# A filter, two mixtures of experts, one planned program: the order of the last layer's slots and a third count product

## The chip, the cores and the metric

One core of one Trainium2 chip runs the whole program in one launch. The metric is device time in microseconds; the median of 3 runs of the kernel before is 1300.23 us (1297.22 to 1307.93).

## The reference

The input x has shape (4, 2496, 256). Three stages follow each other:

1. A filter: a real FFT along the 2496 positions, a product with a complex filter, the inverse FFT. Its output is taken as 9984 tokens of 256 numbers.
2. A first mixture of 8 experts (256 to 1024, relu, 1024 to 256) with greedy capacity. All 9984 x 8 logits are sorted; from the largest down, each free token goes to that expert unless the expert already holds 1248 tokens. 8 x 1248 = 9984, so at the end every expert is full.
3. A second mixture of 8 experts of the same sizes: each token goes to the expert with the largest cosine similarity, and its output is scaled by the softmax weight. There is no capacity, so these experts get unequal numbers of tokens.

```python
logits = x @ w_gate
for idx in np.argsort(-logits.flatten()):
    tok, e = (int(idx) // E, int(idx) % E)
    if assigned[tok] >= 0 or counts[e] >= cap:
        continue
    assigned[tok] = e
    counts[e] += 1
...
expert_idx = np.argmax(logits2, axis=1)
out[mask] = gate_w[mask, None] * (np.maximum(x[mask] @ w1[e], 0.0) @ w2[e])
```

## The kernel before

**Stages.** `Fft` does the filter and writes the tokens to `xs` in memory. `Moe.layers` (from L1576) then works through a fixed list of 46 items, one after the other, on TensorE (PE). An item is a block of up to 512 token rows for one expert: its rows are transposed (L989), multiplied by the expert's first matrix in eight chunks (L1006), passed through relu (L1009 on ScalarE, the remainder L1012 on VectorE), and multiplied by the second matrix (L1024), two chunks behind. All matrices are split into a high and a low part (L957 on ScalarE, L958 on VectorE), because every product is made of three float32r products.

**Items, counted from 0, in the kernel before.** Items 0 to 16 are the first mixture's easy part: expert "full" in three blocks, then the seven "known" experts with 2 x 384 rows each. Then come the seven "late" blocks of 480 rows (the rest of each expert), mixed with "slots". A slot is 512 rows of one expert of the second mixture; which expert and which rows is read from a table on the chip. The order is: late 1 and 2 (items 17, 18), four slots slA (19 to 22), late 3 and 4 (23, 24), three slots slC (25 to 27), late 5, 6, 7 (28 to 30), five slots slM (31 to 35), eight slots slB (36 to 43), two half slots slS (44, 45). With the reference's inputs these slots hold every token, and the general loops of `rest` (L1693) don't run: the trace has 84 scatters into `out`, 20 x 4 + 2 x 2.

**The search.** Which tokens belong to a late block is known only when the greedy phases are done (`Greedy.phase`, L729; seven searches `Greedy.search`, L515). Phase k ends with the expert's number `ei` (L802). A search is a chain of small VectorE steps with a TensorE product between them, which adds counts over partitions: four coarse products (L535), one of the coarse remainder `sg` (L561), two of 63 thresholds (L576).

**The lists.** For each block `compact` (L864) turns a mask into row numbers `ids` and flags `val` (L908, L910). `Moe.listing` calls it in order: full, known 1 to 7, late 1 to 7. Known lists wait until the item is at most `SOON` ahead; late lists are made as soon as their expert is known. GpSimd (POOL) then gathers the rows (L1204), two items ahead.

**Routes and tables.** When the items of a group (an entry of `full + known` or of `late`) have left TensorE, `route` (L1359) finds the second mixture's expert for up to 12 tiles of 128 tokens and scatters their rows with GpSimd into `ys` (L1435). Behind certain groups `table_a` (L1292) makes the next table: it looks for experts with 512 rows not taken yet. Groups are routed one after the other. After the last group come `table_b` (L1312), `pads` (16 scatters of filler rows) and `table_s`. A slot's weights (L940, L950) and rows (L1213) are loaded through SP's queue once its table is there, the rows of slB only when the pads are done.

**What sets the order.** The program is written out by a planner in Python that keeps an estimated clock for TensorE, ScalarE and VectorE. In `beside` (L1647), after each piece of TensorE work, it lets background generators take a step: rows and weights, then `routes`, `lists` and `greedy`, as long as VectorE's estimated backlog is small. If TensorE's next item needs something that isn't planned yet, `need` (L1613) pulls the generator until it is there. The rows of item n + 1 are needed when item n has had its fourth chunk (`columns`, called for c in (3, 5)), its weights when it starts. Each engine then executes its part in the order so written.

Of the kernel before, what the change touches and what calls it, by code (L numbers as in the profile page):

```python
# [11 lines left out]
F32 = mybir.dt.float32  # L12
F32R = mybir.dt.float32r
F16 = mybir.dt.float16
# [4 lines left out]
ALU = mybir.AluOpType  # L19
AX = mybir.AxisListType  # L20
# [6 lines left out]
CAP = 1248  # L27
# [6 lines left out]
LATE = CAP - CUT  # L34
# [9 lines left out]
G0 = 42  # L44
SLACK = 1.5
SOON = 8

GT = 12
BEHIND = 2
# [380 lines left out]
class Greedy:  # L430
# [84 lines left out]
    def search(s, mh):  # L515


        nc, c = s.nc, s.c
        V = nc.vector
        need = c['st'][:, 2 * NLEV + 1, :]  # L520
        junk = s.t([128, 702], F16, "m2")
        junk2 = s.t([128, 702], F16, "junk2")
        thr = s.t([128, 3], F32, "thr", bufs=3)
        V.tensor_copy(thr, c['st'][:, 2 * NLEV, :])
        for k in range(NLEV):
            cn = s.t([128, 3], F16, "cn", bufs=2)
            with nc.allow_low_precision(reason="integer counts up to 702 are exact in float16"):
                nc.scalar.activation(junk2, mh, AF.Sign, bias=thr[:, 2:3], scale=1.0, accum_out=cn[:, 2:3])
                for j in (0, 1):
                    V.tensor_scalar(junk, mh, thr[:, j:j + 1], None, op0=ALU.is_ge, op1=ALU.add, accum_out=cn[:, j:j + 1])  # L530
            D = s.t([128, 3], F32, "D", bufs=2)
            V.tensor_tensor(D, thr, c['st'][:, NLEV + k, :], ALU.add)
            yield (1.5, 0.2, 0.87) if k == 0 else (1.65, 0.4, 0.87)
            pc = s.P([128, 3], F32, "gs")
            nc.tensor.matmul(pc, c['o16'], cn, start=True, stop=True)  # L535
            ge = s.t([128, 3], F32, "ge", bufs=2)
            sc = s.t([128, 1], F32, "sc", bufs=2)
            V.scalar_tensor_tensor(ge, pc, 1.0, need, op0=ALU.mult, op1=ALU.is_ge, accum_out=sc)
            th2 = s.t([128, 3], F32, "thr", bufs=3)
            V.scalar_tensor_tensor(th2, c['st'][:, k, :], sc, D, op0=ALU.mult, op1=ALU.add)  # L540
            thr = th2

        base = s.t([128, 1], F32, "Tb")
        up = s.t([128, 1], F32, "Tu")
        sg = s.t([128, 1], F16, "sg")
        V.tensor_scalar(base, thr[:, 0:1], -5.0, None, op0=ALU.add)
        V.tensor_scalar(up, base, -1.0, -4.5, op0=ALU.mult, op1=ALU.add)
        with nc.allow_low_precision(reason="integer counts up to 702 are exact in float16"):
            nc.scalar.activation(junk2, mh, AF.Sign, bias=up, scale=1.0, accum_out=sg)
        yield (0.6,)  # L550
        m2 = s.t([128, 702], F32, "m2")
        V.scalar_tensor_tensor(m2, mh, base, s.K3.rearrange("p a b -> p (a b)"), op0=ALU.subtract, op1=ALU.add)
        yield (0.95,)
        V.scalar_tensor_tensor(m2, m2, 5.0, m2, op0=ALU.is_lt, op1=ALU.mult)
        yield (0.9,)
        top = s.t([128, 8], F32, "top")
        V.max(top, m2)
        yield (0.9, 0.0, 0.87)
        nd = s.t([128, 1], F32, "nd")
        pa = s.P([128, 1], F32, "gs")  # L560
        nc.tensor.matmul(pa, c['o16'], sg, start=True, stop=True)  # L561
        V.tensor_scalar(nd, pa, -0.5, float(CAP - 8 * 702), op0=ALU.mult, op1=ALU.add)
        s.T = s.t([128, 1], F32, "T")
        V.memset(s.T, 1.0)
        for k in range(2):
            th = s.t([128, 63], F32, "th")
            V.tensor_scalar(th, c['j63'], 2.0 ** (-4 - 6 * k), s.T, op0=ALU.mult, op1=ALU.add)
            cm = s.t([128, 63, 8], F16, "cc")
            V.tensor_tensor(cm, top[:, None, :].to_broadcast([128, 63, 8]), th[:, :, None].to_broadcast([128, 63, 8]), ALU.is_ge)
            yield (0.8,)  # L570
            cn = s.t([128, 63], F16, "cn6")
            with nc.allow_low_precision(reason="integer counts up to 8 are exact in float16"):
                V.tensor_reduce(cn, cm, axis=AX.X, op=ALU.add)
            yield 0.6
            pc = s.P([128, 63], F32, "gs")
            nc.tensor.matmul(pc, c['o16'], cn, start=True, stop=True)  # L576
            sc = s.t([128, 1], F32, "sc", bufs=2)
            V.tensor_scalar(th, pc, nd, None, op0=ALU.is_ge, op1=ALU.add, accum_out=sc)
            V.scalar_tensor_tensor(s.T, sc, 2.0 ** (-4 - 6 * k), s.T, op0=ALU.mult, op1=ALU.add)
        s.cnt = s.t([128, 1], F32, "cnt")  # L580
        V.tensor_scalar(th[:, 0:8], top, s.T, None, op0=ALU.is_ge, op1=ALU.add, accum_out=s.cnt)
        V.scalar_tensor_tensor(s.cnt, sg, 0.5, s.cnt, op0=ALU.mult, op1=ALU.add)
        V.tensor_scalar(s.cnt, s.cnt, 351.0, None, op0=ALU.add)

        s.ok = s.t([128, 1], F32, "ok")
        V.tensor_scalar(s.ok, base, 0.0, None, op0=ALU.is_gt)
        s.ov = s.t([128, 1], F32, "ov")
        V.scalar_tensor_tensor(s.ov, top[:, 7:8], 1.0, s.ok, op0=ALU.is_ge, op1=ALU.mult)
        V.tensor_tensor(s.T, s.T, base, ALU.add)
        V.tensor_scalar(s.T, s.T, 1024.0, None, op0=ALU.mult)  # L590
# [438 lines left out]
class Moe:  # L1029
# [2 lines left out]
    NA = 4  # L1032
    NC = 3
    NM = 5
    NB = 8
    NS = 2
    NX = 48

# [19 lines left out]
    def listing(s):  # L1058
        g = s.greedy
        yield from g.compact(("full", 0), *g.first, CAP)  # L1060
        for k in range(1, NE):
            yield from s.wait_for(g.ei, ("known", k), s.G)
            while s.it < 2 * k + 1 - SOON and not s.force:
                yield 1.0
            yield from g.known(k)
        for ph in range(1, NE):
            yield from s.wait_for(g.ei, ("late", ph), s.G)
            yield from g.late(ph)

    def wait_for(s, got, key, gen):  # L1070
# [370 lines left out]
    def plan(s):  # L1441
        nc, d = s.nc, s.d
        s.items, s.sets = [], []
        V = nc.vector

        def known1(key):
            def f():
                yield from s.wait_for(s.greedy.ei, key, s.G)
                return s.greedy.ei[key][0:1]
            return f  # L1450

        def known2(name, k):
            def f():
                yield from s.table_ready(name)
                return getattr(s, name)[0:1, 0, k:k + 1]
            return f

        def place(name, k):
            def f():
                yield from s.table_ready('padded' if name == 'slB' else name)  # L1460
                return getattr(s, name), k
            return f


        full = [[(("full", 0), FULL)]]
        known = [[(("known", k), KNOWN) for k in range(a, min(a + 2, NE))] for a in (1, 3, 5, 7)]
        late = [[(("late", k), (LATE,)) for k in q] for q in ((1, 2), (3, 4), (5, 6, 7))]
        s.st = {}
        ng = itertools.count()

        def first(groups):
            for lists in groups:
                g, t = next(ng), 0
                for key, parts in lists:
                    s.sets.append(dict(i0=len(s.items), known=known1(key), w1=d['w1m'], w2=d['w2m'], w2x=d['w2x'], engs=(V, V)))
                    k = 0
                    for T in parts:
                        n = [128] * (T // 128) + [T % 128] * (T % 128 > 0)
                        s.items.append(dict(set=len(s.sets) - 1, x=[], list=key, k=k, g=g, t=t, n=n, last=False))
                        k += len(n)  # L1480
                        t += len(n)
                s.items[-1]['last'] = True

        def slots(name, N, w):
            for k in range(N):
                s.sets.append(dict(i0=len(s.items), known=known2(name, k), w1=d['w1n'], w2=d['w2n'], w2x=None, engs=(V, V)))
                s.items.append(dict(set=len(s.sets) - 1, x=[], place=place(name, k), n=[128] * w))

        first(full + known)
        n = len(full + known)  # L1490
        s.tables = {n - 2: ('slA', s.NA), n: ('slC', s.NC), n + 1: ('slM', s.NM)}
        for k, name, N in ((0, 'slA', s.NA), (1, 'slC', s.NC), (2, 'slM', s.NM)):
            first(late[k:k + 1])
            slots(name, N, 4)
        slots('slB', s.NB, 4)
        slots('slS', s.NS, 2)
        s.groups = next(ng)

    def done1(s, q, t, m, last=False):
# [502 lines left out]
```

## Time and profile before

| | |
|---|---|
| median of 3 runs | 1300.23 us (1297.22, 1300.23, 1307.93) |
| profiled execution | 1316.35 us |
| its span in the trace | 1314.6 us |
| TensorE busy | 1219.6 us, 93% of the span |
| VectorE, ScalarE, GpSimd busy | 65%, 51%, 33% |
| mean granted TensorE clock | 0.971 |

How to read it: TensorE's matmuls are pipelined, so its busy share shows where it had work, and not that it ran at its peak. A slice or window in which its busy time or its granted clock falls is one in which it waited. ScalarE's first relu of an item is a good mark of the item's start, since there are eight per item in a fixed order; the distance between two such marks is what an item took.

### The profile page before, as it was taken

To read this page: it belongs to the slowest core of one execution; us is meant where nothing else is said; L and a number is where in the kernel's file an instruction comes from. 1 tells how busy PE (TensorE), PEld (TensorE's weight loads), DVE (VectorE), ACT (ScalarE), POOL (GpSimd) and SP (SyncE) were. 2 spreads that over 40 slices of the span, in tenths; PEclk is the share of its full clock that TensorE was granted. 3 is DMA by queue.
4 is the path that set the end of the run, shared out by engine and by line. 5 is a ranking of instruction groups with operands and counts; after the bars stand their busy time and mean duration, and the time that the engine had idled before them with its cause. 6 is when DMAs were issued, how large, how long until landed. Compare 5 with 4: busy or idle time off the path is not lost.

```text
span 1314.6 us, 23468 instructions
## 1 busy us (share of the span) xinstructions
PE 1219.6 (93%) x7893; PEld 1057.5 (80%) x7893; DVE 858.0 (65%) x2061; ACT 665.2 (51%) x1407; POOL 429.8 (33%) x955
## 2 busy tenths in 40 slices
PE   7998999699999989989899999987899899999996
PEld 7565545489999989989788999876799899999996
DVE  2578767578787877887767778763456464445543
ACT  2666656455465564554455456433454444545443
POOL 1334300303363533736147221621114731211112
PEclk9998999799999999999999999997899999999998
DMA  7876667541243322421545443422533654443420
GB/s 238 253 237 216 208 209 223 176 125 47 68 130 91 111 74 57 132 86 57 154 143 180 129 130 114 125 90 76 159 116 126 195 163 130 140 146 131 126 91 24
DMA packets 124044, 178.26 MB, mean 136 GB/s; under 512 B 29383, under 2 KB 88763, under 8 KB 123645
## 3 DMA queue, kind: packets, MB, share of 16 engines
q1 hardware_dynamic: 111131, 143.33, 36.1%
q0 software_dynamic: 12480, 33.17, 7.4%
q8 instruction: 64, 1.05, 0.3%
q14 instruction: 79, 0.65, 0.2%
q10 hardware_dynamic: 290, 0.07, 0.0%
HBM read 137.32 MB, written 39.99 MB: 135 GB/s over the span
## 4 chain that ended last, share of the span: by engine, by line
PE 48%; DVE 7%; issue 4%; POOL 2%; ACT 2%; DMA 1%; POOLq 0%; DVEq 0%; ACTq 0%
PE kp_b L1024 23%; PE kp_a L1006 23%; PE kp_a L989 2%; DVE k_hl L1012 2%; DVE k_w1l L958 1%; DMA k_xg<-xs,g_ids 1%; ACT k_hh L1009 1%; POOL ys L1435 0%; POOL out L1435 0%; DVE k_w L958 0%; ACT g_le L899 0%; POOL k_xg L1204 0%; DVE g_m L530 0%; ACT k_w1h L957 0%; DMA k_raw<-w1m 0%
## 5 line engine op out<-in xcount | busy, mean ns | idle before, releaser
L1024 PE MATMUL kp_b<-k_w,k_hh 128*128 128x256 f32 (+2 forms) x2624 | 505.5, 289 | 3.1 <-ACT k_y L1506 3.1
L1024 PEld LDWEIGHTS kp_b<-k_w,k_hh 128*128 128x128 f32 (+1 forms) x2624 | 422.0, 190 | 17.1 <-ACT k_y L1506 3.7
L1009 ACT ACTIVATE k_hh<-kp_a 128x512 fp32r<-128x512 f32 (+3 forms) x368 | 201.4, 548 | 433.8 <-PE kp_a L1006 350.5
L1012 DVE SCALAR_TENSOR_TENSOR k_hl<-kp_a,k_hh 128x512 fp32r<-128x512 f32 (+3 forms) x368 | 228.4, 624 | 247.3 <-ACT k_hh L1009 196.1
L1024 PE MATMUL kp_b<-k_w,k_hl 128*128 128x256 f32 (+2 forms) x1312 | 372.3, 284 | 1.7 <-DVE g_oth L836 1.0
L1006 PE MATMUL kp_a<-k_xh,k_w1h 128*128 128x512 f32 (+3 forms) x736 | 274.0, 373 | 9.8 <-DVE k_hl L1012 6.0
L1006 PE MATMUL kp_a<-k_xl,k_w1h 128*128 128x512 f32 (+3 forms) x736 | 274.0, 373 | 0.9 <-issue 0.9
L1024 PEld LDWEIGHTS kp_b<-k_w,k_hl 128*128 128x128 f32 (+1 forms) x1312 | 248.1, 189 | 1.5 <-DVE g_oth L836 1.2
L1006 PE MATMUL kp_a<-k_xh,k_w1l 128*128 128x512 f32 (+3 forms) x736 | 213.5, 371 | 5.3 <-DVE k_w1l L958 5.3
L1435 POOL DMA_INDIRECT out<-k_xg,k_y x84 | 88.5, 1054 | 281.0 <-ACT k_xg L1523 262.4
L1006 PEld LDWEIGHTS kp_a<-k_xh,k_w1h 128*128 128x128 f32 x736 | 140.6, 191 | 21.0 <-DVE k_hl L1012 7.2
L1006 PEld LDWEIGHTS kp_a<-k_xh,k_w1l 128*128 128x128 f32 x736 | 137.3, 190 | 23.4 <-DVE k_w1l L958 6.1
L1006 PEld LDWEIGHTS kp_a<-k_xl,k_w1h 128*128 128x128 f32 x736 | 140.3, 191 | 11.3 <-issue 1.7
L1204 POOL DMA_INDIRECT k_xg<-xs,g_ids x80 | 84.8, 1060 | 180.6 <-issue 117.8
L958 DVE TENSOR_TENSOR k_w<-k_raw,k_w 128x1024 fp32r<-128x1024 f32 (+2 forms) x75 | 91.5, 1222 | 14.5 <-ACT k_w L957 11.3
L958 DVE TENSOR_TENSOR k_w1l<-k_raw,k_w1h 128x1024 fp32r<-128x1024 f32 x74 | 90.2, 1224 | 14.0 <-ACT k_w1h L957 13.4
L1435 POOL DMA_INDIRECT ys<-k_y,m_pi x80 | 83.2, 1040 | 33.4 <-POOL m_sp L1434 18.3
L302 POOL TENSOR_TENSOR v<-sw,ff 128x512 f32<-128x512 f32 x40 | 50.9, 1273 | 97.1 <-ACT sw L300 96.5
L1507 POOL COPY m_L<-k_y 128x8 f32<-128x8 f32 x80 | 19.2, 262 | 190.9 <-ACT k_y L1506 188.5
L957 ACT CAST k_w<-k_raw 128x1024 fp32r<-128x1024 f32 (+2 forms) x75 | 78.5, 1049 | 0.0
L957 ACT CAST k_w1h<-k_raw 128x1024 fp32r<-128x1024 f32 x74 | 76.4, 1042 | 2.4 <-DMA k_raw<-w1m 2.4
L992 DVE TENSOR_TENSOR k_xl<-kp_a,k_xh 128x512 fp32r<-128x512 f32 (+3 forms) x92 | 56.9, 619 | 24.3 <-ACT k_xh L991 24.2
(344 smaller groups left out, 1504.3 us busy)
## 6 DMA issues: line engine op xcount, KB each, us to landing
k_raw<-w1n SPq DMA_DIRECT2D x44, 512.0 KB
k_raw<-w2n SPq DMA_DIRECT2D x44, 512.0 KB
k_raw<-w1m SPq DMA_DIRECT2D x30, 512.0 KB
k_raw<-w2m SPq DMA_DIRECT2D x30, 512.0 KB
k_y<-ys SPq DMA_DIRECT2D x84, 132.0 KB
ff<-ff SPq DMA_DIRECT2D x40, 256.0 KB
xs<-yt SPq DMA_DIRECT2D x42, 234.0 KB
w2m<-w2mt SPq DMA_DIRECT2D x16, 512.0 KB
```

The costliest lines, as they stand in the source:

```text
L302: nc.gpsimd.tensor_tensor(r2(v), r2(sw), bc(ff[:, 256:512]), ALU.mult)
L957: s.nc.scalar.copy(hi, src)
L958: f = lambda: eng.tensor_tensor(lo, src, hi.bitcast(F32), ALU.subtract)
L989: nc.tensor.transpose(p[:, 128 * k:128 * k + n], tt[:n, 128 * c:128 * c + 128], s.ident[:n, :n])
L992: late(lambda: nc.vector.tensor_tensor(b, p[:, :T], a.bitcast(F32), ALU.subtract), T)
L1006: nc.tensor.matmul(p[:, :T], w[:, c, f0:f0 + 128], x[:, c, :T], start=q == 0, stop=q == 5)
L1009: nc.scalar.activation(hh[:, :T], p[:, :T], AF.Relu)
L1012: nc.vector.scalar_tensor_tensor(o, a, 0.0, b, op0=ALU.max, op1=ALU.subtract), T, (id(H), f))
L1024: nc.tensor.matmul(p[:m, :n], h[:, t0:t0 + m], w[:, f, :], start=f == 0 and q == 0 and (n > 256 or b % 2 == 0), stop=f == 7 and q == 2 and ...
L1204: s.nc.gpsimd.indirect_dma_start(out=x[:m], out_offset=None, in_=s.d['xs'], in_offset=bass.IndirectOffsetOnAxis(ap=ids[:m], axis=0))
L1435: st = s.nc.gpsimd.indirect_dma_start(out=out, out_offset=bass.IndirectOffsetOnAxis(ap=idx, axis=0), in_=src, in_offset=None, **k)
L1507: nc.gpsimd.tensor_copy(q['L2'][:m, :, t:t + 1], y[:m, 256:264][:, :, None])
```

## The change

It does three things. In `search` the product of `sg` is no longer made by itself: `sg` is copied into a 64th column beside the 63 counts, and the need `nd` is read from that column of the first of the two products. In `listing` a late list is made only when its item is at most `LSOON` = 5 ahead. In `plan` the late groups become (1, 2), (3, 4), (5, 6), (7), so there is one more route; two of the five slM slots come ahead of late 5; and behind group (5, 6) a fourth table slN of two slots is made, which leaves six slots for slB. The order is then: late 1, 2 (17, 18), slA (19 to 22), late 3, 4 (23, 24), slC (25 to 27), slM (28, 29), late 5, 6, 7 (30 to 32), slM (33 to 35), slN (36, 37), slB (38 to 43), slS (44, 45).

```diff
--- before.py
+++ after.py
@@ -44,6 +44,7 @@
 G0 = 42
 SLACK = 1.5
 SOON = 8
+LSOON = 5
 
 GT = 12
 BEHIND = 2
@@ -555,11 +556,8 @@
         yield (0.9,)
         top = s.t([128, 8], F32, "top")
         V.max(top, m2)
-        yield (0.9, 0.0, 0.87)
+        yield (1.0,)
         nd = s.t([128, 1], F32, "nd")
-        pa = s.P([128, 1], F32, "gs")
-        nc.tensor.matmul(pa, c['o16'], sg, start=True, stop=True)
-        V.tensor_scalar(nd, pa, -0.5, float(CAP - 8 * 702), op0=ALU.mult, op1=ALU.add)
         s.T = s.t([128, 1], F32, "T")
         V.memset(s.T, 1.0)
         for k in range(2):
@@ -568,14 +566,17 @@
             cm = s.t([128, 63, 8], F16, "cc")
             V.tensor_tensor(cm, top[:, None, :].to_broadcast([128, 63, 8]), th[:, :, None].to_broadcast([128, 63, 8]), ALU.is_ge)
             yield (0.8,)
-            cn = s.t([128, 63], F16, "cn6")
+            cn = s.t([128, 64], F16, "cn6")
+            V.tensor_copy(cn[:, 63:64], sg)
             with nc.allow_low_precision(reason="integer counts up to 8 are exact in float16"):
-                V.tensor_reduce(cn, cm, axis=AX.X, op=ALU.add)
+                V.tensor_reduce(cn[:, 0:63], cm, axis=AX.X, op=ALU.add)
             yield 0.6
-            pc = s.P([128, 63], F32, "gs")
+            pc = s.P([128, 64], F32, "gs")
             nc.tensor.matmul(pc, c['o16'], cn, start=True, stop=True)
             sc = s.t([128, 1], F32, "sc", bufs=2)
-            V.tensor_scalar(th, pc, nd, None, op0=ALU.is_ge, op1=ALU.add, accum_out=sc)
+            if k == 0:
+                V.tensor_scalar(nd, pc[:, 63:64], -0.5, float(CAP - 8 * 702), op0=ALU.mult, op1=ALU.add)
+            V.tensor_scalar(th, pc[:, 0:63], nd, None, op0=ALU.is_ge, op1=ALU.add, accum_out=sc)
             V.scalar_tensor_tensor(s.T, sc, 2.0 ** (-4 - 6 * k), s.T, op0=ALU.mult, op1=ALU.add)
         s.cnt = s.t([128, 1], F32, "cnt")
         V.tensor_scalar(th[:, 0:8], top, s.T, None, op0=ALU.is_ge, op1=ALU.add, accum_out=s.cnt)
@@ -1032,7 +1033,9 @@
     NA = 4
     NC = 3
     NM = 5
-    NB = 8
+    MFIRST = 2
+    NN = 2
+    NB = 6
     NS = 2
     NX = 48
 
@@ -1060,11 +1063,13 @@
         yield from g.compact(("full", 0), *g.first, CAP)
         for k in range(1, NE):
             yield from s.wait_for(g.ei, ("known", k), s.G)
-            while s.it < 2 * k + 1 - SOON and not s.force:
+            while s.it < s.wanted["known", k] - SOON and not s.force:
                 yield 1.0
             yield from g.known(k)
         for ph in range(1, NE):
             yield from s.wait_for(g.ei, ("late", ph), s.G)
+            while s.it < s.wanted["late", ph] - LSOON and not s.force:
+                yield 1.0
             yield from g.late(ph)
 
     def wait_for(s, got, key, gen):
@@ -1464,7 +1469,7 @@
 
         full = [[(("full", 0), FULL)]]
         known = [[(("known", k), KNOWN) for k in range(a, min(a + 2, NE))] for a in (1, 3, 5, 7)]
-        late = [[(("late", k), (LATE,)) for k in q] for q in ((1, 2), (3, 4), (5, 6, 7))]
+        late = [[(("late", k), (LATE,)) for k in q] for q in ((1, 2), (3, 4), (5, 6), (7,))]
         s.st = {}
         ng = itertools.count()
 
@@ -1481,19 +1486,25 @@
                         t += len(n)
                 s.items[-1]['last'] = True
 
-        def slots(name, N, w):
-            for k in range(N):
+        def slots(name, ks, w):
+            for k in ks:
                 s.sets.append(dict(i0=len(s.items), known=known2(name, k), w1=d['w1n'], w2=d['w2n'], w2x=None, engs=(V, V)))
                 s.items.append(dict(set=len(s.sets) - 1, x=[], place=place(name, k), n=[128] * w))
 
         first(full + known)
         n = len(full + known)
-        s.tables = {n - 2: ('slA', s.NA), n: ('slC', s.NC), n + 1: ('slM', s.NM)}
-        for k, name, N in ((0, 'slA', s.NA), (1, 'slC', s.NC), (2, 'slM', s.NM)):
-            first(late[k:k + 1])
-            slots(name, N, 4)
-        slots('slB', s.NB, 4)
-        slots('slS', s.NS, 2)
+        s.tables = {n - 2: ('slA', s.NA), n: ('slC', s.NC), n + 1: ('slM', s.NM), n + 2: ('slN', s.NN)}
+        first(late[:1])
+        slots('slA', range(s.NA), 4)
+        first(late[1:2])
+        slots('slC', range(s.NC), 4)
+        slots('slM', range(s.MFIRST), 4)
+        first(late[2:])
+        slots('slM', range(s.MFIRST, s.NM), 4)
+        slots('slN', range(s.NN), 4)
+        slots('slB', range(s.NB), 4)
+        slots('slS', range(s.NS), 2)
+        s.wanted = {z['list']: k for k, z in reversed(list(enumerate(s.items))) if 'list' in z}
         s.groups = next(ng)
 
     def done1(s, q, t, m, last=False):
```

## Rows read from the trace of the kernel before

**Rows 1.** the page, part 1: engine, busy us (share of the span), instructions
```profile
PE 1219.6 (93%) x7893; PEld 1057.5 (80%) x7893; DVE 858.0 (65%) x2061; ACT 665.2 (51%) x1407; POOL 429.8 (33%) x955
```

**Rows 2.** waits of PE over the span: us in total, times, longest
```profile
PE kp_a L989 <- DMA k_xg<-xs,g_ids: 23.5, 11, 8.6
```

**Rows 3.** one window: PE, PEld, DVE, ACT, POOL busy, granted clock, DMA share, GB/s
```profile
885.00:900.00 15.00, 4.78 (x22) 3.54 (x22) 3.61 (x23) 2.33 (x10) 3.88 (x4) 0.55 0.37 112
```

**Rows 4.** ScalarE timeline, first relu of items 28, 29, 30, 31, 36 and 37
```profile
874.07 0.57 ACT L1009 ACTIVATE k_hh<-kp_a 128x480 fp32r<-128x480 f32 x1 [2.11 <-PE kp_a L1006]
...
918.12 0.56 ACT L1009 ACTIVATE k_hh<-kp_a 128x480 fp32r<-128x480 f32 x1
...
947.32 0.57 ACT L1009 ACTIVATE k_hh<-kp_a 128x480 fp32r<-128x480 f32 x1 [1.28 <-PE kp_a L1006]
...
970.41 0.60 ACT L1009 ACTIVATE k_hh<-kp_a 128x512 fp32r<-128x512 f32 x1 [2.30 <-PE kp_a L1006]
...
1092.90 0.60 ACT L1009 ACTIVATE k_hh<-kp_a 128x512 fp32r<-128x512 f32 x1 [1.26 <-PE kp_a L1006]
...
1116.09 0.60 ACT L1009 ACTIVATE k_hh<-kp_a 128x512 fp32r<-128x512 f32 x1 [1.26 <-PE kp_a L1006]
```

**Rows 5.** VectorE timeline: expert number of phase 6, end of late 6's list
```profile
878.29 0.15 DVE L802 TENSOR_SCALAR g_ei<-g_rst 128x1 int32<-128x1 f32 x1 [2.96 <-DVEq L795]
...
890.62 0.22 DVE L910 TENSOR_SCALAR g_val<-c_it,g_n 128x4 f32<-128x4 f32 x1
```

**Rows 6.** TensorE timeline: first transpose of late 6's rows
```profile
893.82 0.47 PE L989 MATMUL kp_a<-ident,k_xg 128*128 128x128 f32 x1 [6.02 <-DMA k_xg<-xs,g_ids]
```

**Rows 7.** VectorE timeline, phase 0: the maximum and the thresholds that follow
```profile
207.16 0.89 DVE L557 MAX8 g_top<-g_m 128x8 f32<-128x702 f32 x1
...
209.34 0.25 DVE L567 TENSOR_SCALAR g_th<-c_j,g_T 128x63 f32<-128x63 f32 x1
```

**Rows 8.** the instructions of L561: ns least/median/most, first and last start
```profile
L561 PE MATMUL gps<-g_sg,c_o x7: 177/178/178, 207.9 to 823.4; 128*128 128x1 f16 x7
```

**Rows 9.** ScalarE timeline: first relu of items 18, 19 and 20
```profile
624.14 0.57 ACT L1009 ACTIVATE k_hh<-kp_a 128x480 fp32r<-128x480 f32 x1 [2.21 <-PE kp_a L1006]
...
655.43 0.60 ACT L1009 ACTIVATE k_hh<-kp_a 128x512 fp32r<-128x512 f32 x1 [5.74 <-PE kp_a L1006]
...
684.64 0.60 ACT L1009 ACTIVATE k_hh<-kp_a 128x512 fp32r<-128x512 f32 x1 [2.11 <-PE kp_a L1006]
```

**Rows 10.** VectorE timeline: positions of group 3, late 3's mask, table slA written
```profile
589.44 0.17 DVE L1421 TENSOR_TENSOR m_pi<-m_pf,m_val 128x12 int32<-128x12 f32 x1
...
591.09 0.24 DVE L848 SCALAR_TENSOR_TENSOR g_lm<-g_asg,g_left 117x88 f32<-117x88 f32 x1
...
628.78 0.17 DVE L1277 CAST m_slslA<-m_ek 128x4 int32<-128x4 f32 x1
```

**Rows 11.** VectorE timeline: positions of group 6, two parts of table slM
```profile
839.90 0.17 DVE L1421 TENSOR_TENSOR m_pi<-m_pf,m_val 128x12 int32<-128x12 f32 x1
...
859.47 0.17 DVE L1250 TENSOR_TENSOR_SCAN m_cum<-one,m_nt 128x8 f32<-128x8 f32 x1
...
867.83 0.17 DVE L1277 CAST m_slslM<-m_ek 128x5 int32<-128x5 f32 x1
```

**Rows 12.** TensorE timeline: first transposes of item 28, in item 27's fourth chunk
```profile
859.03 0.57 PE L989 MATMUL kp_a<-ident,k_xg 128*128 128x128 f32 x4
```

**Rows 13.** the page, part 5: the scatters of routed rows
```profile
L1435 POOL DMA_INDIRECT ys<-k_y,m_pi x80 | 83.2, 1040 | 33.4 <-POOL m_sp L1434 18.3
```

**Rows 14.** ScalarE timeline: first relu of item 25
```profile
802.85 0.60 ACT L1009 ACTIVATE k_hh<-kp_a 128x512 fp32r<-128x512 f32 x1 [0.44 <-PE kp_a L1006]
```

**Rows 15.** VectorE timeline, last group: its reciprocal and its positions
```profile
989.35 0.22 DVE L1378 RECIPROCAL m_sqn<-m_sqn 128x12 f32<-128x12 f32 x1
...
997.75 0.17 DVE L1421 TENSOR_TENSOR m_pi<-m_pf,m_val 128x12 int32<-128x12 f32 x1
```

**Rows 16.** SP's queue: rows of the first slB slot
```profile
1062.87 0.33 SPq L1213 DMA_DIRECT2D k_y<-ys  x1
```

## The prediction

> **What bounds the kernel now.** TensorE, by its own work: it is busy 93% of the span [rows 1], so what can be won are its waits. The list of waits puts first the transposes that wait for gathered rows: 23.5 us in 11 waits [rows 2]. The table of windows shows where most of that lies: from 885 to 900 us TensorE works 4.78 of 15 us and VectorE 3.61, so no engine is the bound there [rows 3]. Then I read the relu marks, since they give the price of a stretch with everything in it. Late 6 comes 44.05 us behind late 5 and late 7 29.20 us behind late 6, while late 7 itself takes 23.09 us and an undisturbed slot 23.19 us [rows 4]. So the two items lose 20.96 + 6.11 = 27.1 us.
>
> The rows below say why. Phase 6 of the search gives its expert only at 878.29, when late 5 already runs, and late 6's list is done at 890.62 [rows 5]; its first transpose starts at 893.82, behind the gather [rows 6]. The search and the lists were pulled to the end at the last moment, and TensorE stood in front of the transposes.
>
> **What the change removes.** Two slots ahead of late 5 move late 6 and 7 back by 2 x 23.19 = 46.4 us [rows 4]. The list was late by far less than that, so even a search that ends where it ended is in time. The order of the late lists (at most five items ahead) costs nothing here: late 5 to 7 become items 30 to 32, so their lists may be made from items 25 to 27 on, and one list, pulled, took 890.62 - 878.29 = 12.3 us from the expert's number [rows 5]. **-27.1 us**; bounds -21 (late 7 still waits) and -27.
>
> The joined product: in phase 0 nothing covers the search, since no item can start before the full expert is known. There the maximum ends at 207.16 + 0.89 = 208.05 and the thresholds start at 209.34 [rows 7]. The 1.29 us between hold another stage's evacuation and the wait for the product; the change puts in two copies of one column, each like the smallest VectorE row here, 0.15 us [rows 5]. **-1.0 us**, bounds 0 and -2. In phases 1 to 6 it only ends the search sooner, which pays nothing once late 6 has its 46 us; if a phase were to bound, it would pay there. On TensorE seven products of 0.178 us go [rows 8], and the new route brings two; **-0.8 us**, bounds 0 and -1.2.
>
> The first table, slA, gains by the rule for lists. Today the first slA slot comes 655.43 - 624.14 = 31.29 us behind late 2, 8.2 more than 23.09 [rows 4, 9], since its table is written only at 628.78 [rows 10]. From the group's positions to its table it takes 39.34 us [rows 10], and for slM 27.93 us [rows 11]. Four tiles more explain 4 x (1.04 + 33.4 / 80) = 5.8 us [rows 13]. In the remaining 5.6 us lies late 3's list, which starts at 591.09, just then [rows 10]; it is now made from item 18 on. **-5 us**, bounds 0 and -8.2.
>
> **What it adds.** The first moved slM slot is the disputed term. Item 28 is now a slot, and its rows are wanted where late 5's transposes stand today, at 859.03 [rows 12], 15.04 us ahead of its first relu at 874.07. But group 6 ends with item 24, as today, and its table is written at 867.83 [rows 11]. It can't be left there: the planner pulls the rest of the route when TensorE's order comes to the transposes. Of the table, the second part runs from 859.47 [rows 11]; some sixteen more instructions of about 0.18 us put the cast at 859.47 + 2.9 = 862.4. Nearest is slA, where 655.43 - 628.78 = 26.65 us lie between the cast and the first relu [rows 9, 10]: rows, then weights through SP's queue, then their split on ScalarE and VectorE. 862.4 + 26.65 = 889.0, against 874.07: **+15 us**. Bounds: +20.4 if the cast stays at 867.83, 0 if the route runs ahead of today's. I take the middle one, as the pull is in the code. In SP's queue only that slot's own four row loads and four weight loads stand behind this wait, and the next slot's behind them; TensorE stands in item 27's fourth chunk, with item 27's second matrix behind it.
>
> The second slot behind a late table: 684.64 - 655.43 = 29.21 us, 6.0 more than 23.19 [rows 4, 9]. There the next group's route was pulled as well, and here no group is due: **+2 us**, bounds 0 and +6.
>
> The fourth table. From the end of its last item to its reciprocal a route takes 989.35 - 970.41 = 18.94 us, then 8.40 us to the positions [rows 4, 15], then 27.93 us to the table: 55.3 us; with the search beside it, as for slM, 867.83 - 802.85 = 65.0 us [rows 11, 14]. The first slN slot (item 36) has its first relu 23.09 + 3 x 23.19 = 92.7 us behind late 6's end, and needs 55.3 + 26.65 = 82.0, at most 91.6: **0 us**. Cover is thin; with ten more us of route it would cost those.
>
> Group (7) can be routed only behind slN. Today 1062.87 - 989.35 = 73.5 us lie between the last reciprocal and the first slB rows [rows 15, 16]; with 8 tiles fewer, 8 x 1.46 = 11.7 us less, 61.8. Its reciprocal comes 0 to 18.9 us behind table slN; its squares are done by then, I take 5. 55.3 + 5 + 61.8 + 4 for landing = 126 us behind late 6's end, at most 136. The rows are wanted at 23.09 + 5 x 23.19 - 15.04 = 124.0 us: **+4 us**, bounds 0 and +12. The route's and table's own work lies on VectorE, ScalarE and GpSimd, busy for 65, 51 and 33% [rows 1]; what waits for it is counted above. Filling is no issue: routing the reference's own inputs gives 14 whole blocks of 512 behind late 6, so slN's two are there (4 + 3 + 5 + 2), and six and two remain for slB and slS; the loops of `rest` still don't run.
>
> **Sum.** -27.1 - 1.0 - 0.8 - 5 + 15 + 2 + 4 = -12.9 us, from the profiled execution's 1316.35 us to 1303.4. That execution is 16 us above the median of the runs; I carry the difference over to it: 1300.23 - 12.9 = **1287 us**.
>
> In rows, a wait costs more than its idle time: in the window of the gap the granted clock is 0.55, so mostly the lower of the two levels, 1.2 GHz [rows 3]. The Trainium skill ("TensorE: Matmul & The Clock Gate", Part 1) says that the throttled clock is the default and that activity releases it, which speaks against splitting one gap into three at three tables. By that rule each new gap would also pay its own cold tail; estimated at 1.5 us a gap, the sum would be 1291 us. The marks from slA on which my terms rest have such a tail in them, so I don't add it.
>
> **Rivals.**
> - The tables are in time (slM costs 0 to 5, slB 0): then 1300.23 - 33.9 + 3 = 1269 us. For it: the search ends sooner and takes less of VectorE, so routes run faster. Against: today's table at 867.83 is 9 us behind the place where it will be wanted.
> - Slower: the chain from a group's last item to its table is the new bound, and grows, because late 5's and 6's lists, which must now wait for items 25 and 26, fall beside group 6's route, as late 3's fell beside slA's [rows 10]. Point from which it decides: a chain of over 65 us. Then slM costs 20.4 and 6, slN 6, slB 12, and slA gives nothing: -28.9 + 44.4 = +15.5, 1316 us. For it: 39.34 against 27.93 us [rows 10, 11]. Against: the pull in the fourth chunk caps it.
> - The change doesn't do what it says: the search slips by what it gains, since routes go first in the planner, and late 6 waits again behind the slots. Then the gain is what slA and the joined product give, less slM: about 1300 us. Against: 46.4 us of room.
>
> **Numbers.** Forecast 0.45 (1277 to 1297), tables in time 0.25, slower chain 0.18, no effect 0.12. One per cent, 13 us, is about what can be told from no change: below 1287.2 lie half of the forecast and the second case, 0.47; above 1313.2 two thirds of the third case, 0.12; the rest 0.41. The range leaves out the ends of the second and third cases: 1266 to 1310.
>
> **What would show it.** Late 6 and 7 with relu distances of 23 to 24 us, and no transpose waiting for a gather there. The wait of TensorE in item 27's fourth chunk for slot rows, and of item 28 for its low weights: first relu of item 28 about 38 us behind item 27's, 15 more than a slot's 23.19. Table slA written a few us sooner against late 2's first relu. A short wait for rows in item 37. I am wrong if item 28 comes 24 us behind item 27 (then 1269), if slN or slB slots wait by 10 us each (then slower), or if late 6's list is again the last thing that TensorE waits for.

## The result, and the profile after

The changed kernel takes 1282.14 us (median of 4 runs, 1280.75 to 1284.61) against 1301.88 us before (4 runs), a ratio of 0.9848 with a 95% interval of 0.9802 to 0.9893. The forecast was 1287 us; 19.7 us are gained (13.9 to 25.8 by the interval), and 12.9 were forecast, so the direction and the time came out and the gain was forecast too small. The profiled execution of after took 1284.61 us with a span of 1282.7 us and a mean granted clock of 0.983.

The page, part 1, after (answers to [rows 1]), and TensorE's waits for rows (answers to [rows 2]):

```profile
PE 1213.0 (95%) x7888; PEld 1056.0 (82%) x7888; DVE 864.4 (67%) x2124; ACT 665.1 (52%) x1410; POOL 443.6 (35%) x972
```

```profile
PE kp_a L990 <- DMA k_xg<-xs,g_ids: 8.9, 3, 7.4
PE kp_a L990 <- DMA k_y<-ys: 8.3, 6, 6.1
```

The 23.5 us in 11 waits for gathered tokens have become 8.9 in 3 (the 7.4 are item 0's), and a wait for routed rows (k_y) has grown to 6.1 us at the most. ScalarE's relu marks after, items 27 to 32 and 36 to 37 (answer to [rows 4]):

```profile
836.96 0.60 ACT L1010 ACTIVATE k_hh<-kp_a 128x512 fp32r<-128x512 f32 x1 [2.22 <-PE kp_a L1007]
...
872.59 0.60 ACT L1010 ACTIVATE k_hh<-kp_a 128x512 fp32r<-128x512 f32 x1 [1.39 <-PE kp_a L1007]
...
896.48 0.60 ACT L1010 ACTIVATE k_hh<-kp_a 128x512 fp32r<-128x512 f32 x1 [2.33 <-PE kp_a L1007]
...
920.07 0.57 ACT L1010 ACTIVATE k_hh<-kp_a 128x480 fp32r<-128x480 f32 x1 [2.14 <-PE kp_a L1007]
...
943.00 0.57 ACT L1010 ACTIVATE k_hh<-kp_a 128x480 fp32r<-128x480 f32 x1 [1.26 <-PE kp_a L1007]
...
965.98 0.57 ACT L1010 ACTIVATE k_hh<-kp_a 128x480 fp32r<-128x480 f32 x1 [1.26 <-PE kp_a L1007]
...
1059.76 0.60 ACT L1010 ACTIVATE k_hh<-kp_a 128x512 fp32r<-128x512 f32 x1 [1.29 <-PE kp_a L1007]
...
1083.19 0.60 ACT L1010 ACTIVATE k_hh<-kp_a 128x512 fp32r<-128x512 f32 x1 [1.29 <-PE kp_a L1007]
```

Late 6 and 7 (now items 31, 32) come 22.93 and 22.98 us behind their forerunners, where they came 44.05 and 29.20 [rows 4]. The price stands at the first moved slot, item 28: 35.63 us instead of a slot's 23.43. Why it waits, on VectorE (phase 6's expert and table slM, answers to [rows 5, 11]), on TensorE (first transpose of item 28's rows), and in windows (answer to [rows 3]; columns as there; the last one lies inside the first two):

```profile
838.57 0.15 DVE L803 TENSOR_SCALAR g_ei<-g_rst 128x1 int32<-128x1 f32 x1 [3.11 <-DVEq L796]
...
847.40 0.17 DVE L1282 CAST m_slslM<-m_ek 128x5 int32<-128x5 f32 x1
```

```profile
851.51 0.45 PE L990 MATMUL kp_a<-ident,k_y 128*128 128x128 f32 x1 [6.14 <-DMA k_y<-ys]
```

```profile
840.00:855.00 15.00, 7.46 (x41) 5.89 (x41) 4.65 (x22) 3.44 (x8) 8.08 (x12) 0.80 0.45 131
855.00:870.00 15.00, 15.00 (x90) 13.61 (x89) 8.23 (x26) 5.71 (x9) 0.00 (x0) 0.85 0.49 152
870.00:885.00 15.00, 14.33 (x94) 12.62 (x94) 11.35 (x24) 10.26 (x24) 6.04 (x8) 1.00 0.72 244
...
851.50:859.30 7.80, 6.38 (x22) 5.17 (x23) 2.25 (x12) 0.59 (x1) 0.00 (x0) 0.50 0.84 242
```

The table is written 10.4 us behind item 27's first relu, its rows are then loaded, and TensorE stands: its waits between the two relu marks add up to 8.2 us. Behind the long one, from 851.50 to 859.30 us, it works again for 6.38 of 7.80 us, but at a granted clock of 0.50, the lower of the two levels (1.2 GHz); from 859.5 us on it has 1.00. The other 4 of the item's 12.2 us are thus not idle time, and a window with a low granted clock is not always one in which TensorE waits, as "How to read it" ahead of the prediction has it: in the one from 855 to 870 us it is busy all of the 15 us, at 0.85. The Trainium skill ("TensorE: Matmul & The Clock Gate", Part 1) says that the throttled clock is the default and that activity releases it; the trace agrees here. The mark's distance holds both parts, as the sum assumed.

Two more things differ from the forecast. Late 2 to the first two slA slots (items 18, 19, 20; answers to [rows 9]) takes 54.8 us instead of 60.5. And every slot takes 23.43 us instead of 23.19 (items 36, 37).

```profile
611.17 0.57 ACT L1010 ACTIVATE k_hh<-kp_a 128x480 fp32r<-128x480 f32 x1 [2.20 <-PE kp_a L1007]
...
640.21 0.60 ACT L1010 ACTIVATE k_hh<-kp_a 128x512 fp32r<-128x512 f32 x1 [2.54 <-PE kp_a L1007]
...
665.94 0.60 ACT L1010 ACTIVATE k_hh<-kp_a 128x512 fp32r<-128x512 f32 x1 [1.61 <-PE kp_a L1007]
```

### The profile page after: what moved, and what is told of

Same layout as the page of the kernel before. It is cut to its first block, busy times and chain, and to the rows that moved or that the text cites. A ratio compares the mean times of both kernels' runs of the same rounds, so it can differ in the third digit from the quotient of the medians.

```text
span 1282.7 us, 23546 instructions
## 1 busy us (share of the span) xinstructions
PE 1213.0 (95%) x7888; PEld 1056.0 (82%) x7888; DVE 864.4 (67%) x2124; ACT 665.1 (52%) x1410; POOL 443.6 (35%) x972
## 4 chain that ended last, share of the span: by engine, by line
PE 60%; issue 16%; DVE 8%; POOL 6%; DMA 6%; ACT 2%; SPq 1%; POOLq 0%; ACTq 0%; DVEq 0%
PE kp_b L1025 25%; PE kp_a L1007 24%; POOL out L1440 3%; PE py L415 2%; PE kp_a L990 2%; DMA xg<-xh 2%; POOL ys L1440 1%; DVE k_hl L1013 1%; PE pz L401 1%; DVE g_m L531 1%; PE pf L296 1%; DMA X<-xh 1%; PE pq L227 1%; POOL v L303 1%; DVE k_w1l L959 1%
```

## The experiments

The theory at the start: the order gains the late waits and pays at slM; the joined product and the rule for lists give little. Rivals: the search alone now comes in time, so the order pays nothing; or the gain is an effect of addresses, since the new order's buffers shift the relu outputs by 32 bytes, and each slot changed by 0.24 us. Runs e1 to e8 are from one chip, where the kernel before takes 1313.7 to 1314.9 us, e9 to e12 from another, where it takes 1302.4 us; ratios are to the kernel before on the same chip. They are worked out from the single runs, so they can differ a little from the ratio of two medians.

**Addresses: e1, e2, e5.** A buffer that nothing reads is made larger, no instruction is added. It shifts the buffers allocated behind it, among them the relu outputs, which are the stationary operand of the second product (what TensorE holds while the other operand streams past). Within 256 bytes the relu outputs begin at 192 before, 224 after, 0 in e1, 224 in e2 (the kernel before, shifted) and 192 in e5; these offsets are the program's, the traces hold no addresses.

```diff
-        s.spacer = s.t([1, 1], F32, "sp")
+        s.spacer = s.t([1, 16], F32, "sp")[:, 0:1]     # e1, e2 (e5: 64)
```

> The changed kernel with one 4-byte tile made 32 bytes longer, so that the tiles behind it (relu's outputs among them, which TensorE loads as weights in the second product) start at a multiple of 64 bytes again, as in the kernel before; no instruction is added. In the changed kernel's trace a slot late in the list takes 23.43 us, before 23.19 us, with the same work. Theory A, the address: slots go back to 23.19 us, and 3936 products of the second matrix at 2.4 ns each give 9 us back: about 1273 us. Rival, the new order (other queues beside the slots): slots stay at 23.43 us and the time at 1282 us.

> The kernel before with the same tiles shifted by 32 bytes, to where the changed kernel has them. Theory A, the address: slots take 23.43 us and the whole about 9 us more, 1311 us. Rival: no difference, 1302 us and 23.19 us.

> The changed kernel with the same tiles shifted by 224 bytes, so that relu's outputs start at the same place within 256 bytes as in the kernel before (192). e1 put them at 0 within 256 and slots took 23.37 us, not 23.19. Theory, the place within 256 bytes counts: slots take 23.19 us and the ratio to the kernel before falls by 0.18 / 23.4 of the item time, some 6 us, below e1's 0.980: about 0.976. Rival, something else than this address makes 23.19: slots stay at 23.37 and the ratio at 0.980.

Slots take 23.19 us at 192 (e5), 23.43 at 224 (e2), 23.37 at 0 (e1): the address sets the slot. The 9 us that I expected of e1 and e2 were too many, since the late items keep their pace (late 6 takes 22.99 us in after and 22.97 in e5). The address does not make the gain, because after has slower slots than the kernel before, and e5, at the same offset as before, gains 0.0182 of the time. e1: 1289.73 us, ratio 0.9803 (0.9769 to 0.9837); e2: 1320.39 us, 1.0027 (1.0003 to 1.0052), 3.5 us, where 20 full slots of 0.24 us would be 4.8; e5: 1287.30 us, 0.9818 (0.9783 to 0.9853). That e5 is no faster than e1 has a reason of its own, in the last section.

**The order taken out: e3 and e6.** e3 has the joined product and the rule, e6 the joined product alone, both in the old order.

```diff
     NM = 5
-    MFIRST = 2
-    NN = 2
-    NB = 6
+    NB = 8
...
-        late = [... for q in ((1, 2), (3, 4), (5, 6), (7,))]
+        late = [... for q in ((1, 2), (3, 4), (5, 6, 7))]
...                                          # tables and order of the slots as before
-            while s.it < s.wanted["late", ph] - LSOON and not s.force:     # left out in e6 alone
-                yield 1.0
```

> The change without its order: groups, slots and tables as before, with the joined product and the rule that late lists are made at most five items ahead; addresses as in the kernel before. Theory of the prediction: the moved slots are what removes the waits of late 6 and 7, so these stay (44 and 29 us between relu marks), and only the small terms are won, 1.0 + 0.8 + 5: about 1295 us. Rival: the search, which ends 40 us sooner in the changed kernel, would be in time without moved slots: late 6 and 7 at 24 to 28 us, and with the 13 to 19 us that the changed kernel has won by item 20, about 1265 to 1275 us.

> The kernel before with the joined product alone. e3 (join and rule for late lists) won 13 per mille, 16.7 us, where the prediction's working had 6.8. Theory, the join does it: five microseconds less per search mean that all later lists, routes and tables get VectorE sooner, so this kernel wins 10 to 15 us (0.989 to 0.992). Rival, the rule does it: the join wins 2 us (0.9985), as the prediction had it.

e3: 1298.19 us, 0.9872 (0.9841 to 0.9903). e6: 1296.91 us, 0.9893 (0.9852 to 0.9934). ScalarE's relu marks of late 5, 6 and 7 in e3:

```profile
856.94 0.57 ACT L1010 ACTIVATE k_hh<-kp_a 128x480 fp32r<-128x480 f32 x1 [2.11 <-PE kp_a L1007]
...
895.59 0.57 ACT L1010 ACTIVATE k_hh<-kp_a 128x480 fp32r<-128x480 f32 x1 [2.21 <-PE kp_a L1007]
...
928.50 0.57 ACT L1010 ACTIVATE k_hh<-kp_a 128x480 fp32r<-128x480 f32 x1 [1.28 <-PE kp_a L1007]
```

38.65 and 32.91 us: the late waits stay without the order (late 7 comes 94.7 us behind item 27, where it came 96.7 before), so the first rival falls. But e6 gains 14 us with the joined product alone, which I had put at 1.8. Its relu marks of items 18, 19 and 20 show a part:

```profile
612.98 0.57 ACT L1009 ACTIVATE k_hh<-kp_a 128x480 fp32r<-128x480 f32 x1 [2.21 <-PE kp_a L1006]
...
640.12 0.60 ACT L1009 ACTIVATE k_hh<-kp_a 128x512 fp32r<-128x512 f32 x1 [2.59 <-PE kp_a L1006]
...
666.35 0.60 ACT L1009 ACTIVATE k_hh<-kp_a 128x512 fp32r<-128x512 f32 x1 [2.25 <-PE gps L535]
```

53.4 us from late 2 to the second slot, less than after's 54.8, without the rule for lists: what I had put down to the rule comes from the joined product. The later runs bear this out: the same stretch takes 60.7 us with neither (e10), 59.9 with the rule alone (e8), 53.4 with the joined product alone (e7) and 54.4 with both (e5).

**One part taken out of after: e7 (the rule), e8 (the joined product),** at e5's addresses. e7 leaves out the two lines marked above; e8 puts `search` back as it was.

> The changed kernel without the rule for late lists (they are made as soon as their expert is known), addresses as in e5. Prediction's working: table slA comes 5 us later, so about 5 us above e5. If the join did all of e3: the same as e5 within 3 us. If the rule did it: 12 to 15 us above e5.

> The changed kernel with the two count products apart again, addresses as in e5. Prediction's working: 2 us above e5, since late 6 has 46 us of room. If the join did all of e3: 10 to 15 us above e5, and the loss shows in items 10 to 20, not at late 6 and 7.

e7: 1293.57 us, 0.9869 (0.9838 to 0.9899). e8: 1302.80 us, 0.9905 (0.9864 to 0.9946). Against e5 the joined product is worth 0.0087 of the time before here, 11 us, and the rule 0.0051, 6.7 us. The intervals of the rule's pair overlap, and e7's own runs go from 1283.9 to 1294.7. The joined product's pair also differs in stops of the kind told in the last section (items 35 to 37: 57.1 us in e8's profile, 53.9 in e5's), so about 3 of the 11 us may be those.

**The product put back with no reader: e9.**

```diff
-        yield (1.0,)
+        yield (0.9, 0.0, 0.87)              # the planner's step for the product, as before
         nd = s.t([128, 1], F32, "nd")
+        pa = s.P([128, 1], F32, "gs")
+        nc.tensor.matmul(pa, c['o16'], sg, start=True, stop=True)
+        V.tensor_scalar(nd, pa, -0.5, float(CAP - 8 * 702), op0=ALU.mult, op1=ALU.add)
...
             cn = s.t([128, 64], F16, "cn6")     # the join as in after
```

> The changed kernel at the addresses of e5, with the joined product kept, and the seven small products and their seven readings put back where they stood, with no reader (nothing of the computation changes; the reading's result is overwritten). It asks whether the joined product's 11 to 14 us come from the work and the wait that it takes away, or from its being one link less for the search's data. Work and wait (an in-order queue with one more wait in it): as slow as e8, ratio to before 0.989 to 0.992, items 15 to 16 about 20 us apart. Chain of the data only: as e5, ratio 0.980 to 0.983, items 15 to 16 16.3 us apart. My own step for TensorE alone (products of 0.18 us): 1 to 2 us more than e5.

1290.92 us, 0.9900 (0.9871 to 0.9929): as slow as e8 by the ratio. Seven products of 0.18 us and seven readings of 0.15 us are 2.3 us of work, nothing needs their result, and e9 lies 6.8 us above after by the ratios, or 10.0 us by the marks from item 0 to item 28, although its slots are the faster ones (e5's addresses). The relu marks say where it goes. Items 15 and 16, before, e9, after:

```profile
558.65 0.48 ACT L1009 ACTIVATE k_hh<-kp_a 128x384 fp32r<-128x384 f32 x1
...
580.39 0.48 ACT L1009 ACTIVATE k_hh<-kp_a 128x384 fp32r<-128x384 f32 x1
```

```profile
552.36 0.48 ACT L1013 ACTIVATE k_hh<-kp_a 128x384 fp32r<-128x384 f32 x1
...
572.50 0.48 ACT L1013 ACTIVATE k_hh<-kp_a 128x384 fp32r<-128x384 f32 x1
```

```profile
552.70 0.47 ACT L1010 ACTIVATE k_hh<-kp_a 128x384 fp32r<-128x384 f32 x1
...
569.05 0.49 ACT L1010 ACTIVATE k_hh<-kp_a 128x384 fp32r<-128x384 f32 x1 [1.52 <-PE kp_a L1007]
```

21.74, 20.14 and 16.35 us for the same item. ScalarE's and TensorE's timelines inside it, in e9:

```profile
556.82 0.88 ACT L550 ACTIVATE g_junk<-g_mh,g_Tu 128x702 f16<-128x702 f16 x1 [2.25 <-DVE g_R L873]
...
557.70 0.92 ACT L1520 COPY k_y<-kp_b 128x264 f32<-128x264 f32 x3
```

```profile
558.11 0.51 PE L1028 MATMUL kp_b<-k_w,k_hh 128*128 128x264 f32 x2 [2.36 <-ACT k_y L1520]
```

A search step on ScalarE (L550) has to wait 2.25 us for VectorE; the evacuation of the second product's bank is written behind it in ScalarE's queue, and TensorE waits 2.36 us for that bank. Before has the same group, longer: the step waits 2.67 us and TensorE 2.82 us, in the records

```profile
563.12 0.88 ACT L549 ACTIVATE g_junk<-g_mh,g_Tu 128x702 f16<-128x702 f16 x1 [2.67 <-DVE g_R L869]
```

```profile
564.41 0.51 PE L1024 MATMUL kp_b<-k_w,k_hh 128*128 128x264 f32 x2 [2.82 <-ACT k_y L1506]
```

In after the same search step runs before the item's first relu. It waits there too, for 2.12 us, but the evacuation comes only 1.7 us behind its end, and TensorE doesn't wait:

```profile
551.82 0.88 ACT L550 ACTIVATE g_junk<-g_mh,g_Tu 128x702 f16<-128x702 f16 x1 [2.12 <-DVE g_Tu L548]
...
554.38 0.95 ACT L1517 COPY k_y<-kp_b 128x264 f32<-128x264 f32 x3
```

This item holds 3.8 of the 10.0 us. Another 4.7 lie between late 2 and the second slot (59.4 us in e9, 54.8 in after): there TensorE waits 3.38 us for the low part of the weights and 2.88 us for the relu's remainder, both made on VectorE (L962, L1016); in after its waits for parts of the weights are 1.88 and 1.19 us, and none is for the remainder. So the seven products cost mostly by where they push the rest of the search in the written order, and not by their own time. What pushes it is not separated: e9 puts back the products, the readings and the planner's step together. By the code a step of three numbers makes the planner hold the search back until its estimated clock is `SLACK` = 1.5 us past the piece, and a step of one number doesn't; a run with the planner's step and without the products is missing. Nor is the search's data wholly cleared: from item 0 to item 21, in one profile each, e9 is 10.1 us slower than after, but e8 is 13.5.

**The order alone: e10** (join and rule both undone, e5's addresses).

> The new order of slots and the fourth table, with the seven small products made as before and the late lists made as before. If the parts add up, it is e8 (0.9905) without what the rule for lists is worth, so 0.990 to 0.996: rule worth 3 to 6 us means 0.993 to 0.995, rule worth nothing means 0.9905. Late 6 and 7 without a wait (23 to 24 us from relu to relu), item 28 about 35 to 37 us behind item 27, items 18 to 19 about 29 us, because without the joined product slA's route is later.

1287.13 us, 0.9883 (0.9831 to 0.9934): 15.2 us gained, more than the 0.990 to 0.996 that I expected. Relu marks of items 27, 28 and 29:

```profile
845.44 0.60 ACT L1010 ACTIVATE k_hh<-kp_a 128x512 fp32r<-128x512 f32 x1 [2.31 <-PE kp_a L1007]
...
880.80 0.60 ACT L1010 ACTIVATE k_hh<-kp_a 128x512 fp32r<-128x512 f32 x1 [0.99 <-PE kp_a L1007]
...
904.22 0.60 ACT L1010 ACTIVATE k_hh<-kp_a 128x512 fp32r<-128x512 f32 x1 [2.29 <-PE kp_a L1007]
```

35.36 us, then 23.42. From the item ahead of late 5 to late 7, relu to relu, it takes 69.7 us here and took 96.7 before [rows 4, and item 28's 23.43]: -26.9 + 12.2 + 0.2 = -14.5 us, and the medians give -15.2 (8.6 to 22.0 by the interval). Within that the order's own account closes, and after's marks give the same -14.5 with the join.

**The moved slots taken from an earlier table: e4, e11, e12.** slC gets five slots and slM three, none of them ahead of late 5; the place of slots in the order is that of after. e4 at e1's addresses, e11 at e5's; e12 is e11 without the rule.

```diff
-    NC = 3
-    NM = 5
-    MFIRST = 2
+    NC = 5
+    NM = 3
+    MFIRST = 0
```

> The changed kernel with the two slots ahead of late 5 taken from the table before: slC has five slots, slM three (all behind late 7), slN two; addresses as in e1. Theory: item 28's 12 us (35.63 against 23.43 us in the changed kernel) are the wait for the table slM, written at 847.4 us for a slot that wants its rows at 845; with a table that is there 130 us ahead it goes, item 28 comes 24 us behind item 27, and the time is 11 to 12 us below e1. Rival: the wait moves to late 6's list or to the slM slots behind late 7, and the time is that of e1 within 4 us.

> e4 (five slots of table slC, three of slM, none of slM ahead of late 5) at the addresses of e5: slots of 23.19 us instead of 23.37 to 23.43. With 17 slots and 18 other items that would be 4 us less than e4, ratio to before 0.966; if the short waits of engines for nothing that the profile shows come back elsewhere, as they did from e1 to e5, 0.967 to 0.972, no better than e4.

> e11 without the rule that late lists are made at most five items ahead. Rule worth 3 to 6 us, as e6 against e3 and e7 against e5 would have it: ratio 0.969 to 0.972. Rule worth nothing, or only a shift of the wait behind late 2 (27.2 us without, 29.0 with): within 2 us of e11. Items 18 to 19: 27.2 us here, 29.0 to 29.4 in e11.

e4: 1275.41 us, 0.9693 (0.9663 to 0.9723), 14 us less than e1. e11: 1264.33 us, 0.9717 (0.9682 to 0.9751). e12: 1264.35 us, 0.9732 (0.9687 to 0.9776). Relu marks of items 27, 28, 29 in e11:

```profile
837.98 0.60 ACT L1010 ACTIVATE k_hh<-kp_a 128x512 fp32r<-128x512 f32 x1 [2.19 <-PE kp_a L1007]
...
861.17 0.60 ACT L1010 ACTIVATE k_hh<-kp_a 128x512 fp32r<-128x512 f32 x1 [2.19 <-PE kp_a L1007]
...
884.89 0.60 ACT L1010 ACTIVATE k_hh<-kp_a 128x512 fp32r<-128x512 f32 x1 [2.19 <-PE gps L874]
```

The 12.2 us at item 28 are gone: the wait was for table slM, and a table that is there earlier removes it. Beside a kernel before of the same time (1302.37 and 1301.88 us) e11 lies 17.8 us below the changed kernel; 12.2 for the table and some 20 x 0.24 = 4.8 for the addresses of 20 full slots make 17.0. e11's ratio missed my 0.966. That was worked out from e4's on the other chip, which may be the reason; it is not shown. Both kernels beat before and after. The rule for lists gives nothing between e11 and e12 (0.02 us by the medians); from late 2 to the second slA slot it costs 54.66 - 51.76 = 2.9 us, of which 2.6 are still there at item 28 in the two profiles.

## Why the prediction was right, and which terms were not

- **Late 6 and 7, -27.1.** Right: -27.2 by after's marks (69.5 us for late 5 to 7 against 96.7). e3 shows that the order does it: without it 2.0 us go.
- **First moved slM slot, +15.** Right in place and mechanism (rows behind the pulled route, then weights), a little large: +12.2. The table came 10.4 us behind item 27's first relu, 11.8 were taken; from table to relu it took 25.2 us, 26.65 were taken.
- **Second slot, +2; slN, 0; slB, +4.** Measured +0.5 and 0 and 0: items 36 and 38 follow at a slot's distance. The short wait for rows in item 37 that I named didn't come. The slB term was a sum of links that each came out shorter: table slN was written 43.0 us behind late 6's end (55.3 were taken), and the first slB rows were loaded 115.9 us behind it (122 were taken).
- **The joined product, -1.8: the step that failed.** I costed it by its instructions and took the search for covered. In phase 0 that holds: the thresholds now start 208.01 - 207.97 = 0.04 us behind the maximum, before 1.29 [rows 7]. But item 0 starts anywhere between 251.65 and 258.75 us in the fourteen profiles, so that microsecond is not seen. In items 1 to 20, which I held to be covered, it pays most: as item 15 shows, an item's own evacuation waits behind a search step in ScalarE's queue. From item 0 to item 21 the kernels with the join are 16.9 (e6 beside before), 15.1 (e7 beside e10) and 14.8 us (e5 beside e8) ahead of those without, each in one profile; part of that is given back later. By the marks from item 0 to item 28, after is 10.0 us ahead of e9 and 9.6 of e10; the pairs of ratios give 14 (e6 beside before), 11 (e5 beside e8), 7 (after beside e9) and 2 us (e7 beside e10, on two chips). That it is more than 1.8 is shown by e6, whose interval ends at 0.9934, 8.7 us; the exact size is not, and neither is which part of it comes from the planner's step.
- **slA by the rule, -5.** The stretch did get 5.7 us shorter, but from the join (e6, 53.4 us without the rule). Table slA, which I said would come a few us sooner, is written 4.87 us behind late 2's first relu, before 4.64. The rule's four pairs of ratios give -2.8 (e6 to e3), -6.7 (e7 to e5), +2.9 (e10 to e8, on two chips) and -2.0 us (e12 to e11): nothing that can be told from zero.
- **The addresses, not in the sum.** +4.8 us, an estimate from 20 slots of 0.24 us.

The account: -27.2 + 12.2 + 0.5 for the order, about -9 for join and rule, +4.8 for the addresses: -18.7, measured -19.7. It is no independent proof, since the -9 is what lies between the ratios of after and e10, with the addresses taken off; the marks up to item 28, 9.6 and 7 slots of 0.24, would make it -11. Against the forecast's -12.9 the order came out 8.4 us better (-14.5 for -6.1), join and rule together 2 to 4 better (by another cause), and the addresses 4.8 worse. So it is partly luck that 1287 is only 5 us from 1282: a term that the sum did not have took back less than half of what the others had missed.

The rivals: tables in time was wrong for slM and right for slB; the slower chain and no effect are refuted by items 28 to 38 and by e10. The time given for no effect, about 1300 us, was not its sum: -5 - 1.8 + 15 is +8, so 1308. The sum by the rule on cold tails, 1291 us, is further off than 1287, but with other terms out by 8 us the time alone doesn't decide between them; what speaks for leaving the tails out is that the mark at item 28 held its tail and still came out below the +15.

## What to carry to other kernels

A background chain that "nothing waits for" is not free where an engine works off its queue in the written order, as ScalarE does at item 15: look for foreground work that is written behind the chain's steps, and cost a removed step by what moves, not by its own nanoseconds. If a planner writes the order, ask too what the change does to the planner's own steps. Read the price of an item from marks that hold everything in it; the late waits and the two slM slots, taken from marks, came out within 3 us; the slB term, stacked from long links, and the join, counted in instructions, did not. When slots are moved ahead of a stalled item, fill the place from a table that is already there.

## What the hardware showed that was not expected

**Where buffers begin within 256 bytes changes a product's pace.** The same instructions, shifted by 32 bytes: 23.19, 23.43 and 23.37 us a slot at offsets 192, 224 and 0 (e5 and e11; after and e2; e1 and e4). In items 39 to 41 the products of the second matrix start 116.8, 119.2 and 118.2 ns apart on average (e5, after, e1); a slot has 96 of them, and 96 x 2.4 ns are 0.23 of the 0.24 us. Of their operands the relu outputs, the stationary ones, are what the spacer moves. Why is not known; only these three offsets were run.

**On one chip engines stop for nothing that the profile shows.** VectorE's and ScalarE's waits of that kind (total, times, longest) in the profile of before, and in e5's:

```profile
DVE k_hl L1012 <- issue: 46.8, 27, 6.1
```

```profile
DVE k_hl L1013 <- issue: 37.8, 23, 5.8
...
ACT k_hh L1010 <- issue: 27.8, 18, 2.2
...
ACT k_hh L1010 <- remote: 12.6, 3, 5.9
```

All of e1 to e8 have 37.8 to 54.8 us in this row of VectorE; after, e9, e11 and e12 have none and e10 0.5. Where they fall together an item takes 3 to 8 us more: items 21 to 22 (26.40 to 30.90 us in e1 to e7; 23.2 to 23.6 in after and e9, e11, e12) and 33 to 37 (before 28.69 at item 34, e5 28.06 at item 36). So the profile of before, 1316.35 us, is one with such stops, and its comparison with after's overstates the change: 31.7 us between the two profiled executions, 19.7 between the medians. It also explains why e5 has 23.19 us slots and no better time than e1: in the two profiles items 35 to 37 take 53.9 us in e5 and 49.7 in e1, and the 4.2 us use up the 20 x 0.18 = 3.6 that the slots save. That chip runs the kernel before 0.9% slower (1313.65 against 1302.37 us). What the engines wait for there was not tried.
